# Strassen's scheme for the first product of three batches, in a float32 attention and ELU feed-forward kernel

## The chip, the cores and the metric

The kernel runs on one core of a Trainium2 chip. The metric is the device time of one execution in microseconds. Five engines work side by side, each through its own list of instructions: TensorE (PE in the profile, with the weight loads as PEld), VectorE (DVE), ScalarE (ACT), GpSimd (POOL) and SyncE (SP), which starts most transfers. They wait for each other through semaphores.

## The reference, cut to what matters

```python
B, N, C = (4, 6080, 256)                    # q, k, v: four batches
n_tokens, d_model, d_ff = (24320, 256, 2048)

def _attn_ref(q, k, v, tau):
    qn = q / (np.linalg.norm(q, axis=1, keepdims=True) + 1e-06)
    kn = k / (np.linalg.norm(k, axis=1, keepdims=True) + 1e-06)
    s = kn.transpose(0, 2, 1) @ qn / tau    # 256 x 256 per batch: attention over channels
    a = softmax(s)                          # by rows, with 1e-9 under the fraction
    return v @ a

x = _attn_ref(q, k, v, tau).reshape(24320, 256)
h = x @ w_in                                # 256 -> 2048
g = where(h > 0, h, exp(min(h, 0)) - 1)     # ELU
out = g @ w_out                             # 2048 -> 256
```

All of it is float32. w_in and w_out arrive as float64 and are converted on the chip.

## The kernel before

Each batch has its own 256 x 256 attention matrix. The kernel never forms v @ a: it multiplies the matrix into w_in (a tile `pw`, 256 x 2048 per batch, kept as `wp`) and then computes h = v @ wp. So the work per batch is a gram matrix k^T q with the column norms, a softmax, the product of a and w_in, and two large products.

For TensorE every float32 operand x is kept as two float32r tiles: hi, the cast of x, and lo = x - hi. One product is then three matmuls, hi hi, hi lo and lo hi (lines 423 to 425 and 461 to 465). The function `split` (lines 114 and 115) makes the two: a cast on ACT and a subtraction on DVE.

The 6080 tokens of a batch are cut into 12 chunks (8 of 512 and 4 of 496 columns), 48 in all. A chunk takes 16 steps, one for each 128 rows of the hidden layer. In a step `h_item` makes `ph` from `vt` (the chunk of v) and `wp` with 6 matmuls, `elu` makes `e` from it on ACT and DVE, `split_g` makes the pair `g`, and three steps later `out_item` adds g times w_out into the two banks `po` with 6 matmuls. ELU has two forms that alternate in most chunks: Relu(-h), Exp(-.), and a maximum (lines 434 to 436), or Exp, a clamp and a maximum (lines 438 to 440).

The first four chunks are interleaved while the weights are being converted. From then on chunk follows chunk. Side work is entered in a table of steps by hand: the groups of rows of the next batch's gram (load, square, add to `acc`, split, matmuls, which `fine` puts between the second product's matmuls), its softmax, its `pw`. Up to the first steps after the first four chunks, TensorE, DVE and ACT run in program order; after that a scheduler sets the order. The pool "w" has three PSUM banks, "gram" two and "o" three. GpSimd does almost nothing.

## Time and profile before

| What | Value |
|---|---|
| timed runs | 2165.70 and 2166.98 us, median 2166.34 |
| span of the profiled execution | 2163.4 us; the page gives no other time of it, the two timed runs are 2.3 and 3.6 us above it |
| busy share of the span | PE 100%, weight loads 88%, DVE 71%, ACT 68%, GpSimd 0% |
| granted TensorE clock | 1.00 in every stretch |

The rows that the prediction quotes are of five kinds. The page has the busy time of each engine and the chain of work that ended last, with its shares by engine. A row of stretches has a start and an end in us, its length, and for PE, PEld, DVE, ACT and POOL the busy time and the count of instructions, then the granted clock, the DMA share and GB/s. A row of the timeline has start, duration, engine, line, operation and tiles. A row of groups has line, engine, operation, tiles, shape and count, then busy time in us and mean duration in ns, and behind the second bar the idle time before them with what ended it. A row of DMA issues has the number of issues, the size of each and the us until it landed. L with a number is the line of the kernel. Batch 1's chunks begin near 593 us, batch 2's near 1128 and batch 3's near 1663.

### The profile page before, as it was taken

The numbers are of one execution on the slowest core, as the hardware profiler recorded it, in microseconds if no ns is written. First come the engines' busy times: TensorE is split into PE (matmuls) and PEld (weight loads), VectorE is DVE, ScalarE is ACT, GpSimd is POOL, SyncE is SP. The second block draws the span as 40 slices with busy tenths as digits, with TensorE's granted clock in tenths as the row PEclk, the third lists the DMA queues.
The fourth block names the chain that finished last, engine by engine and source line by source line (L and its number), as shares of the span: only waits on it lengthen the run. The fifth ranks groups of instructions, "written<-read, shape, count | busy, mean of one in ns | idle before, by whom it ended". The sixth has DMA issues, their size and how long they took to land.

```text
span 2163.4 us, 27196 instructions
## 1 busy us (share of the span) xinstructions
PE 2158.6 (100%) x10240; PEld 1911.9 (88%) x10240; DVE 1527.0 (71%) x2358; ACT 1469.1 (68%) x2422; POOL 3.3 (0%) x11
## 2 busy tenths in 40 slices
PE   9999999999999999999999999999999999999999
PEld 8888888899888888889988888888998888888998
DVE  7987777778766776776776677667776666666665
ACT  6877777667666666666766666666776666666665
POOL 0000000000000000000000000000000000000000
PEclk9999999999999999999999999999999999999999
DMA  9320222221111111111111112111112000000000
GB/s 357 107 78 30 78 69 68 68 65 49 59 38 50 49 59 49 59 58 46 39 59 39 49 50 68 49 58 49 56 31 67 20 30 27 23 20 11 20 10 20
DMA packets 62532, 120.77 MB, mean 56 GB/s; under 512 B 6208, under 2 KB 16064, under 8 KB 62400
## 3 DMA queue, kind: packets, MB, share of 16 engines
q1 hardware_dynamic: 62256, 118.91, 16.6%
q8 instruction: 80, 1.31, 0.2%
q14 instruction: 52, 0.43, 0.1%
q10 hardware_dynamic: 144, 0.13, 0.0%
HBM read 92.01 MB, written 27.00 MB: 55 GB/s over the span
## 4 chain that ended last, share of the span: by engine, by line
PE 100%; ACT 0%; DVE 0%; issue 0%
PE po L465 15%; PE po L463 15%; PE ph L423 15%; PE po L461 15%; PE ph L424 15%; PE ph L425 15%; PE gram L203 3%; PE gram L549 2%; PE gram L210 1%; PE pw L374 1%; PE pw L373 1%; PE pw L375 1%; PE pe L549 0%; PE pw L370 0%; PE pd L222 0%; PE pt L337 0%
## 5 line engine op out<-in xcount | busy, mean ns | idle before, releaser
L114 ACT CAST g<-e 128x512 fp32r<-128x512 f32 (+1 forms) x768 | 469.6, 611 | 483.5 <-DVE e L440 281.6
L115 DVE TENSOR_TENSOR g<-e,g 128x512 fp32r<-128x512 f32 (+1 forms) x768 | 525.6, 685 | 323.0 <-ACT g L114 295.6
L465 PE MATMUL po<-g,wo 128*128 128x512 f32 (+1 forms) x1536 | 579.3, 377 | 0.0
L463 PE MATMUL po<-g,wo 128*128 128x512 f32 (+1 forms) x1536 | 579.2, 377 | 0.0
L461 PE MATMUL po<-g,wo 128*128 128x512 f32 (+1 forms) x1536 | 578.9, 377 | 0.0
L423 PE MATMUL ph<-vt,wp 128*128 128x512 f32 (+1 forms) x1472 | 555.4, 377 | 0.0
L425 PE MATMUL ph<-vt,wp 128*128 128x512 f32 (+1 forms) x1472 | 554.5, 377 | 0.0
L424 PE MATMUL ph<-vt,wp 128*128 128x512 f32 (+1 forms) x1472 | 554.5, 377 | 0.0
L436 DVE SCALAR_TENSOR_TENSOR e<-e,ph 128x512 f32<-128x512 f32 (+1 forms) x416 | 283.2, 681 | 242.5 <-ACT e L435 241.9
L434 ACT ACTIVATE e<-ph 128x512 f32<-128x512 f32 (+1 forms) x416 | 246.6, 593 | 129.1 <-PE ph L425 114.4
L461 PEld LDWEIGHTS po<-g,wo 128*128 128x128 f32 x1536 | 290.3, 189 | 37.9 <-DVE scr L478 0.2
L463 PEld LDWEIGHTS po<-g,wo 128*128 128x128 f32 x1536 | 290.3, 189 | 37.8
L465 PEld LDWEIGHTS po<-g,wo 128*128 128x128 f32 x1536 | 290.7, 189 | 34.8 <-DVE g L115 0.3
L424 PEld LDWEIGHTS ph<-vt,wp 128*128 128x128 f32 x1472 | 278.2, 189 | 36.2
L425 PEld LDWEIGHTS ph<-vt,wp 128*128 128x128 f32 x1472 | 278.2, 189 | 36.1
L423 PEld LDWEIGHTS ph<-vt,wp 128*128 128x128 f32 x1472 | 278.2, 189 | 36.1
L435 ACT ACTIVATE e<-e 128x512 f32<-128x512 f32 (+1 forms) x416 | 261.3, 628 | 12.6
L440 DVE TENSOR_TENSOR e<-ph,e 128x512 f32<-128x512 f32 (+1 forms) x352 | 240.6, 684 | 10.4
L438 ACT ACTIVATE e<-ph 128x512 f32<-128x512 f32 (+1 forms) x352 | 207.9, 591 | 31.1 <-PE ph L425 29.2
L439 DVE TENSOR_SCALAR e<-e 128x512 f32<-128x512 f32 (+1 forms) x352 | 147.0, 418 | 20.7 <-ACT e L438 20.6
L182 DVE TENSOR_TENSOR acc<-acc,sq 128x1024 f32<-128x1024 f32 x84 | 102.6, 1221 | 12.2 <-ACT sq L181 11.1
L203 PE MATMUL gram<-qk 128*128 128x512 f32 x268 | 101.6, 379 | 0.0
(134 smaller groups left out, 1183.1 us busy)
## 6 DMA issues: line engine op xcount, KB each, us to landing
raw<-in_q_dram SPq DMA_DIRECT2D x76, 256.0 KB, 2.7
raw<-in_k_dram SPq DMA_DIRECT2D x76, 256.0 KB, 3.0
v<-in_v_dram SPq DMA_DIRECT2D x32, 512.0 KB, 3.6
out_dram<-o SPq DMA_DIRECT2D x56, 256.0 KB, 2.1
v<-in_v_dram SPq DMA_DIRECT2D x16, 496.0 KB, 3.5
out_dram<-o SPq DMA_DIRECT2D x31, 248.0 KB, 2.1
wraw<-w_scr SPq DMA_DIRECT2D x12, 512.0 KB, 3.2
room<-in_q_dram SPq DMA_DIRECT2D x16, 256.0 KB, 5.2
```

The lines of the kernel that those rows point to most:

```text
L114: nc.scalar.copy(hi, src)
L115: nc.vector.tensor_sub(lo, src, hi.bitcast(F32))
L423: nc.tensor.matmul(ph[:, 0:n], wp[kt][:, 0, fs], hi, start=(kt == 0), stop=False)
L424: nc.tensor.matmul(ph[:, 0:n], wp[kt][:, 0, fs], lo, start=False, stop=False)
L425: nc.tensor.matmul(ph[:, 0:n], wp[kt][:, 1, fs], hi, start=False, stop=(kt == KT - 1))
L434: nc.scalar.activation(ev, pv, AF.Relu, scale=-1.0)
L435: x = nc.scalar.activation(ev, ev, AF.Exp, scale=-1.0)
L436: y = nc.vector.scalar_tensor_tensor(ev, ev, -1.0, pv, op0=ALU.add, op1=ALU.max)
L440: y = nc.vector.tensor_tensor(ev, pv, ev, op=ALU.max)
L461: nc.tensor.matmul(o, wo[:, f, 0, ds], hi, start=first(c, f), stop=False)
L463: nc.tensor.matmul(o, wo[:, f, 1, ds], hi, start=False, stop=False)
L465: nc.tensor.matmul(o, wo[:, f, 0, ds], lo, start=False, stop=last(c, f))
```

## The change

For batches 1 to 3 the first product is no longer computed step by step. Four steps (512 rows of the hidden layer) are one unit, `fq`, and the unit's product is cut in 2 x 2 blocks: the product of weights and attention into A11, A12, A21, A22 (two halves of the 256 channels and two of the 512 rows) and the chunk of v into B11, B12, B21, B22 (two halves of the channels and two of the tokens). Strassen's scheme (in Winograd's form) then needs seven block products instead of eight: A11 B11, A12 B21, S3 T3, S2 T2, S1 T1, S4 B22 and A22 T4. The S are sums of A blocks and the T sums of B blocks. Each block product is 6 matmuls of 256 (or 248) columns.

- The sums S and T are made on GpSimd (`s_sum` once per unit of weights and batch, `t_sum` once per chunk), and split in hi and lo like everything else: T and the B blocks are cast on GpSimd, the S on GpSimd or ACT.
- The four results of a unit share partial sums. A11 B11 goes to `bank_a` and is copied on ACT into a second bank `bank_b` (one of two, `b_0` and `b_1`), in which S2 T2, S1 T1 and S4 B22 are accumulated one after the other; between them ACT copies the state of the bank to `u2` and `u4` in SBUF. S3 T3 and then A22 T4 go to `bank_e`, and DVE adds its two states to u4 and u2. So e11 comes from bank_a, e12 from bank_b, e21 from u2 and e22 from u4.
- All steps use the ELU form with Relu and Exp. The cast of g, which ACT did, is done by GpSimd.
- Between the products stand eight pieces of the second product (`multiply_out`), of the unit before. The second product itself has the same matmuls as before.
- All five engines run in program order in this part. Side work is a list of tasks with assumed costs, from which `spend` takes what fits a budget at given places in a unit; matmuls of the side work go between those of the second product (`beside`). The assumed costs are numbers of the code, not measurements shown here. Adding to `acc` and some casts may go to either of two engines.
- Some tiles change their buffers: `aT` shares that of `acc`, `cv` that of `sq`, g is made in pairs with three buffers for four.

Three places show how the instructions stand now. On PE, one step of a 512-column chunk of batch 3 before: `ph` is the first product, `po` the second.

```order
L423 MATMUL ph<-vt_15129,wp_0_13661 128x512
L424 MATMUL ph<-vt_15129,wp_0_13661 128x512
L425 MATMUL ph<-vt_15129,wp_0_13661 128x512
L423 MATMUL ph<-vt_15129,wp_1_13662 128x512
L424 MATMUL ph<-vt_15129,wp_1_13662 128x512
L425 MATMUL ph<-vt_15129,wp_1_13662 128x512
L461 MATMUL po_0_15001<-g,wo 128x512
L463 MATMUL po_0_15001<-g,wo 128x512
L465 MATMUL po_0_15001<-g,wo 128x512
L461 MATMUL po_1_15002<-g,wo 128x512
L463 MATMUL po_1_15002<-g,wo 128x512
L465 MATMUL po_1_15002<-g,wo 128x512
```

On PE after, the first part of a unit of batch 3: `bank_a`, `bank_e` and `b_` are block products, with `t_` and `s_` the tiles of T and of the weights (some B blocks lie in a free place of an `s_` tile).

```order
L1093 MATMUL bank_a<-s_5093,s_4870 128x256 x6
L1093 MATMUL bank_e<-t_5094,s_4870 128x256 x6
L1116 MATMUL po_0_16291<-g_16539,wo 128x512
L1117 MATMUL po_0_16291<-g_16539,wo 128x512
L1118 MATMUL po_0_16291<-g_16539,wo 128x512
L1116 MATMUL po_1_16307<-g_16539,wo 128x512
L1117 MATMUL po_1_16307<-g_16539,wo 128x512
L1118 MATMUL po_1_16307<-g_16539,wo 128x512
L1093 MATMUL b_5086<-t_5094,s_4870 128x256 x6
L1093 MATMUL bank_a<-s_4774,s_4870 128x256 x6
L1116 MATMUL po_0_16697<-g_16599,wo 128x512
L1117 MATMUL po_0_16697<-g_16599,wo 128x512
```

The first product now comes in groups of six narrow matmuls, and S2 T2 into `b_5086` has two block products and two outs ahead of it, during which ACT has to copy bank_a there.

On ACT, a piece of batch 3 before, with ELU's two forms (L434 and L435, L438) and the cast of g (L114).

```order
L114 CAST g<-e 128x512
L438 ACTIVATE e<-ph 128x512
L114 CAST g<-e 128x512
L434 ACTIVATE e<-ph 128x512
L435 ACTIVATE e<-e 128x512
L114 CAST g<-e 128x512
L438 ACTIVATE e<-ph 128x512
```

On ACT after, one unit of batch 3 and the first instruction of the next: `held` has the tiles of u2, e12 and e21, `e_e_5091` is e11, `e_e_5092` e22 and `e_u_5090` u4.

```order
L1455 COPY b_5086<-bank_a 128x512
L1468 COPY held<-b_5086 128x512
L1175 ACTIVATE e_e_5091<-bank_a 128x512
L1176 ACTIVATE e_e_5091<-e_e_5091 128x512
L1476 COPY e_u_5090<-b_5086 128x512
L1175 ACTIVATE e_e_5092<-e_u_5090 128x512
L1176 ACTIVATE e_e_5092<-e_e_5092 128x512
L1175 ACTIVATE held<-b_5086 128x512
L1176 ACTIVATE held<-held 128x512
L1175 ACTIVATE held<-held 128x512
L1176 ACTIVATE held<-held 128x512
L1455 COPY b_5085<-bank_a 128x512
```

The casts are gone, the copies L1455, L1468 and L1476 are new, and the copy for a unit stands behind the last Exp of the unit before.

On GpSimd before, its last instructions: a constant and one memset for each of three batches.

```order
masks.py:199 AFFINE_SELECT ident<-ident 128x128
L169 MEMSET raw_23_4109 128x2x256
L169 MEMSET raw_23_8546 128x2x256
L169 MEMSET raw_23_13108 128x2x256
L891 UNCONDITIONAL_BRANCH
```

On GpSimd after, the end of one unit of batch 3 (the last cast of g), the sums and casts of T for the next chunk, and the casts of g of the unit in which they stand.

```order
L1182 CAST g_18250<-held 128x2x256
L1018 TENSOR_TENSOR tt_18292<-v_18260 128x256
L1019 TENSOR_TENSOR tt_18292<-v_18260 128x256
L1026 CAST t_4714<-tt_18292 128x2x256
L1020 TENSOR_TENSOR tt_18292<-tt_18292,v_18260 128x256
L1021 TENSOR_TENSOR tt_18292<-v_18260,tt_18292 128x256
L1026 CAST t_4714<-tt_18292 128x2x256
L1182 CAST g_18327<-e_e_5091 128x2x256
L1182 CAST g_18363<-e_e_5092 128x2x256
L1182 CAST g_18327<-held 128x2x256
L1182 CAST g_18363<-held 128x2x256
```

Four sums and two casts for T (`tt_`, `t_`) now stand once per chunk ahead of the cast of e11.

The diff, cut to what the prediction speaks of:

```diff
-        aT = work.tile([P, 2, KT, C], F32R, tag="aT", bufs=1, name=f"aT_{b}")
+        aT = work.tile([P, 2, KT, C], F32R, tag="acc", bufs=1, name=f"aT_{b}")
...
-    for i in range(M * FT + LAG, len(steps) + LAG):
-        take(i)
...
+    MATRICES = ("A11", "A22", "A12", "S1", "S2", "S3", "S4")
...
+    def s_sum(b, fq, k):
+        a21, a11, a22, a12, s1, s2, s3, s4 = (x_of(b, fq, y, y + 1) for y in range(8))
+        add, sub = nc.gpsimd.tensor_add, nc.gpsimd.tensor_sub
+        (
+            lambda: add(s1, a21, a22),
+            lambda: sub(s2, s1, a11),
+            lambda: sub(s3, a11, a21),
+            lambda: sub(s4, a12, s2),
+        )[k]()
...
+    def spend(engine, budget, now):
+        order = [(engine, 0), (engine, 1), *((x, y) for x in SHARED.get(engine, ()) for y in range(2)), (engine, 2), (engine, 3)]
+        for key in order:
+            queue = queues[key]
+            while queue and queue[0].ready(now, 0):
+                t = queue[0]
+                cost = t.cost if key[0] == engine else t.cost[engine]
+                if cost > budget:
+                    break
+                queue.pop(0)
...
+    def t_sum(c, k):
...
+            lambda: sub(t1, b12, b11),
+            lambda: sub(t3, b22, b12),
+            lambda: add(t2, t3, b11),
+            lambda: sub(t4, b21, t2),
...
+    def t_hi(c, k):
+        hn = half_of(c)
+        nc.gpsimd.tensor_copy(t_groups[c % 2][:, k : k + 2, 0, 0:hn], state["tt", c][:, k : k + 2, 0:hn])
+
+    def t_lo(c, k):
+        hn = half_of(c)
+        t = t_groups[c % 2][:, k : k + 2]
...
+    def product(bank, c, fq, a, t, begin=False):
+        hn = half_of(c)
+        w, m = s_tiles[fq][:, MATRICES.index(a)], operands[c, t]
+        hi, lo = (in_turns(m[:, x, 0:hn]) for x in range(2))
+        for j in range(2):
+            js = slice(j * P, j * P + P)
+            for k, (x, y) in enumerate(((0, hi), (0, lo), (1, hi))):
+                nc.tensor.matmul(
+                    bank[:, j, 0:hn],
+                    w[:, x, js],
+                    y,
+                    start=(begin and j == 0 and k == 0),
+                    stop=(j == 1 and k == 2),
+                    skip_group_check=True,
+                )
...
+    def multiply_out(count, now):
+        for _ in range(count):
+            if not outs:
+                return
+            item = outs.pop(0)
+            if item is None:
+                continue
+            for _ in out_matmuls(*item):
+                beside(now)
...
+    outs += [None] * 4
...
+    def relu_exp(e, h):
+        nc.scalar.activation(e, h, AF.Relu, scale=-1.0)
+        nc.scalar.activation(e, e, AF.Exp, scale=-1.0)
+
+    def largest(e, h):
+        nc.vector.scalar_tensor_tensor(e, e, -1.0, h, op0=ALU.add, op1=ALU.max)
+
+    def hi_part(g, half, e, hn):
+        nc.gpsimd.tensor_copy(g[:, :, 0, half, 0:hn], e)
+
+    def lo_part(g, half, e, hn):
+        nc.vector.tensor_sub(g[:, :, 1, half, 0:hn], e, g[:, :, 0, half, 0:hn].bitcast(F32))
...
+        x = task(SP, 0, lambda: vraw.__setitem__(d, load_v(d)), when=t + PERIOD, level=0)
+        for k in range(4):
+            x = task(POOL, 0.65, lambda k=k: t_sum(d, k), [x], when=t + PERIOD, level=0)
+            if k % 2 == 1:
+                y = task(POOL, 0.65, lambda k=k: t_hi(d, k - 1), [x], when=t + PERIOD, level=0)
+                task(DVE, 0.685, lambda k=k: t_lo(d, k - 1), [y], when=t + PERIOD, level=0)
+        for k, when in enumerate((2 * PERIOD, 3 * PERIOD, 3 * PERIOD + 1)):
+            y = task(POOL, 0.35, lambda k=k: b_hi(d, k), [x], when=t + when, level=0)
+            task(DVE, 0.415, lambda k=k: b_lo(d, k), [y], level=0)
...
+    PACE = PERIOD * 23 / NG
...
+                    adds.append(task(ADD, {DVE: 0.685, POOL: 1.19}, add, [s], level=0))
...
+        x = task(ACT, 1.9, root, [pn], level=1)
...
+        e = {name: t[:, :, 0:hn] for name, t in e_tiles.items()}
+        bank_a = ps.tile([P, 2, HF], F32, tag="w", bufs=WB, name="bank_a")
+        product(bank_a, c, fq, "A11", "B11", True)
+        bank_b = banks_b[u % 2]
+        va, vb = bank_a[:, :, 0:hn], bank_b[:, :, 0:hn]
+        nc.scalar.copy(vb, va)
+        bank_e = ps.tile([P, 2, HF], F32, tag="w", bufs=WB, name="bank_e")
+        ve = bank_e[:, :, 0:hn]
+        product(bank_e, c, fq, "S3", "T3", True)
+        multiply_out(2, now)
+        if before is not None:
+            before()
+        spend(ACT, 1.9, now)
+        spend(POOL, 4.3, now)
+        spend(DVE, 2.5, now)
+        product(bank_b, c, fq, "S2", "T2")
+        product(bank_a, c, fq, "A12", "B21")
+        multiply_out(1, now)
+        nc.scalar.copy(e["u2"], vb)
+        product(bank_b, c, fq, "S1", "T1")
+        relu_exp(e["e11"], va)
+        largest(e["e11"], va)
+        g1 = work.tile([P, 2, 2, 2, HF], F32R, tag="g", bufs=3, name="g1")
+        hi_part(g1, 0, e["e11"], hn)
+        spend(POOL, 1.3, now + 2)
+        multiply_out(2, now)
+        nc.scalar.copy(e["u4"], vb)
+        nc.vector.tensor_add(e["u4"], ve, e["u4"])
+        product(bank_b, c, fq, "S4", "B22")
+        spend(ACT, 1.25, now + 2)
+        lo_part(g1, 0, e["e11"], hn)
+        spend(DVE, 1.0, now + 2)
+        multiply_out(1, now)
+        product(bank_e, c, fq, "A22", "T4")
+        relu_exp(e["e22"], e["u4"])
+        largest(e["e22"], e["u4"])
+        multiply_out(2, now)
+        g2 = work.tile([P, 2, 2, 2, HF], F32R, tag="g", bufs=3, name="g2")
+        hi_part(g2, 1, e["e22"], hn)
+        nc.vector.tensor_add(e["u2"], ve, e["u2"])
+        relu_exp(e["e12"], vb)
+        relu_exp(e["e21"], e["u2"])
+        lo_part(g2, 1, e["e22"], hn)
+        largest(e["e12"], vb)
+        hi_part(g1, 1, e["e12"], hn)
+
+        def before(e=e, g1=g1, g2=g2, hn=hn):
+            largest(e["e21"], e["u2"])
+            hi_part(g2, 0, e["e21"], hn)
+            lo_part(g1, 1, e["e12"], hn)
+            lo_part(g2, 0, e["e21"], hn)
+
+        for y, g in ((2, g1), (0, g2)):
+            for j in range(2):
+                for dt in range(DT):
+                    outs.append((c, 4 * fq + y + j, g[:, j], dt))
```

More of the change, by code (lines that the diff above doesn't have):

```diff
@@ L284, in norms @@
                 )
+    def norms(parts):
+        pn = ps.tile([P, 2, C], F32, tag="w", bufs=WB, name="pn")
+        for _ in norm_matmuls(parts, pn):
+            pass
         W = C + 2 * KT
@@ L862, in channel_attention_then_elu_ffn, with __init__, ready @@
     in_order.close()
-    for i in range(M * FT + LAG, len(steps) + LAG):
-        take(i)
+    ACT, DVE, POOL, PE, SP, CAST, ADD = "act", "dve", "pool", "pe", "sp", "cast", "add"
+    queues = {(e, level): [] for e in (ACT, DVE, POOL, PE, SP, CAST, ADD) for level in range(4)}
+    class Task:
+        def __init__(self, fn, deps, when):
+            self.fn, self.deps, self.when, self.done, self.cost = fn, deps, when, None, 0.0
+        def ready(self, now, gap):
+            return self.when <= now and all(d.done is not None and d.done + gap <= now for d in self.deps)
@@ new lines, in task @@
+    def task(engine, cost, fn, deps=(), when=0, level=1):
+        t = Task(fn, tuple(d for d in deps if d is not None), when)
+        t.cost = cost
+        queues[engine, level].append(t)
+        return t
+    SHARED = {ACT: (CAST,), DVE: (ADD,), POOL: (CAST, ADD)}
+    def spend(engine, budget, now):
[8 more added lines that the diff above has]
+                queue.pop(0)
+                budget -= cost
+                if key[0] == engine:
+                    t.fn()
+                else:
+                    t.fn({ACT: nc.scalar.copy, DVE: nc.vector, POOL: nc.gpsimd.tensor_copy if key[0] == CAST else nc.gpsimd}[engine])
+                t.done = now
@@ new lines, in channel_attention_then_elu_ffn, with beside @@
+    running = []
+    def beside(now):
+        while True:
+            if not running:
+                for level in range(3):
+                    queue = queues[PE, level]
+                    if queue and queue[0].ready(now, 2):
+                        running.append((queue[0], queue.pop(0).fn()))
+                        break
+                else:
+                    return
+            t, parts = running[0]
+            if next(parts, None) is not None:
+                return
+            t.done = now
+            running.clear()
@@ L868 @@
+    before()
+    now = PERIOD * len(units)
+    while outs:
+        multiply_out(1, now)
+        spend(ACT, 9, now)
+    for queue in queues.values():
+        assert not queue
+    in_order.close()
 _INS = ["q", "k", "v", "tau", "moe_w_in", "moe_w_out"]
```

442 lines of the change are left out of this document (403 added, 39 removed).

## The prediction

> **What bounds the kernel now.** I read the page from the top: the busy times, the 40 slices, the chain that ended last.
>
> ```profile
> span 2163.4 us, 27196 instructions
> ...
> PE 2158.6 (100%) x10240; PEld 1911.9 (88%) x10240; DVE 1527.0 (71%) x2358; ACT 1469.1 (68%) x2422; POOL 3.3 (0%) x11
> ...
> PEclk9999999999999999999999999999999999999999
> ...
> PE 100%; ACT 0%; DVE 0%; issue 0%
> ```
>
> The chain is TensorE from end to end, at full granted clock. A busy PE alone proves little, since its rows overlap; the chain and the pace of its starts do. So next the stretches of batches 1, 2 and 3 (one row each), and the starts of matmuls in the timeline: the first and the last of 58 in a row with 512 columns, of 30 with 496, then one with 256 and its successor.
>
> ```profile
> 593.00:1128.00 535.00, 535.00 (x2555) 474.45 (x2554) 378.53 (x583) 363.71 (x600) 0.73 (x1) 1.00 0.16 51
> 1128.00:1663.00 535.00, 535.00 (x2556) 474.42 (x2555) 378.47 (x583) 363.65 (x600) 0.73 (x1) 1.00 0.16 51
> 1663.00:2163.00 500.00, 496.63 (x2326) 439.15 (x2324) 309.60 (x504) 314.30 (x531) 0.00 (x0) 1.00 0.06 20
> ```
>
> ```profile
> 1699.68 0.38 PE L423 MATMUL ph<-vt,wp 128*128 128x512 f32 x1
> ...
> 1711.98 0.38 PE L461 MATMUL po<-g,wo 128*128 128x512 f32 x1
> ...
> 2153.19 0.37 PE L423 MATMUL ph<-vt,wp 128*128 128x496 f32 x1
> ...
> 2159.25 0.37 PE L465 MATMUL po<-g,wo 128*128 128x496 f32 x1
> ...
> 1004.52 0.27 PE L210 MATMUL gram<-qk 128*128 128x256 f32 x1
> 1004.63 0.38 PE L465 MATMUL po<-g,wo 128*128 128x496 f32 x1
> ```
>
> 12.30 us over 57 starts is 0.2158 us for 512 columns, 6.06 over 29 is 0.209 for 496, and a 256-column matmul holds its successor for 0.11. In the batch rows PE is busy throughout, DVE 71% and ACT 68%. Only less PE work shortens this kernel, as long as the others keep up.
>
> **The change, part by part.** *PE.* I call a quarter of a chunk's first product (4 of its 16 steps) a unit: 36 chunks x 4 = 144 units, of which 96 have 512 columns and 48 have 496. A unit issued 24 matmuls for the first product and 24 for the second. Now the first takes 7 products x 2 halves x 3 = 42 matmuls of 256 (or 248) columns. A long run of such narrow matmuls, each with weights of its own, is not in the trace. The nearest is in the norms: two of 256 columns, then four of 2 columns, whose weight loads stand in the second fence.
>
> ```profile
> 519.18 0.38 PE L274 MATMUL pn<-acc_split,ones_r 128*128 128x256 f32 x2
> ```
>
> ```profile
> 519.29 0.53 PEld L278 LDWEIGHTS pn<-ones_r,acc_split 128*128 128x128 f32 x4
> ...
> L278 PEld LDWEIGHTS pn<-ones_r,acc_split 128*128 128x128 f32 x12 | 1.6, 192 | 0.0
> ```
>
> Four loads of 0.192 in 0.53 us follow each other every (0.53 - 0.192)/3 = 0.113 us although their matmuls are nearly empty. So a narrow matmul costs 0.109 by L210's pace, or up to 0.113 if the loads set it; below that nothing speaks for 256, and for 248 in proportion 0.1056. I take 0.111 for both, because loads and matmuls come out nearly equal.
> 512: before 48 x 0.2158 = 10.36, after 24 x 0.2158 + 42 x 0.111 = 9.84, saved 0.52; x 96 = 50. 496: before 10.03, after 9.68, saved 0.35; x 48 = 17. Together 67 us, between 55 (all at 0.113) and 86 (0.109 and 0.1056). Gram, softmax and the product of weights and attention keep their matmuls.
>
> *The other engines.* Their prices:
>
> ```profile
> L434 ACT ACTIVATE e<-ph 128x512 f32<-128x512 f32 x288 | 171.8, 596 | 81.2 <-PE ph L425 71.3
> L435 ACT ACTIVATE e<-e 128x512 f32<-128x512 f32 x288 | 182.4, 633 | 9.0
> L114 ACT CAST g<-e 128x512 fp32r<-128x512 f32 x512 | 315.1, 616 | 328.2 <-DVE e L440 186.8 <-DVE e L436 141.2
> L487 ACT COPY o<-po 128x512 f32<-128x512 f32 x56 | 31.9, 588 | 4.2 <-PE po L465 3.1
> L440 DVE TENSOR_TENSOR e<-ph,e 128x512 f32<-128x512 f32 x224 | 154.7, 691 | 7.2
> L115 DVE TENSOR_TENSOR g<-e,g 128x512 fp32r<-128x512 f32 x512 | 353.2, 690 | 216.5 <-ACT g L114 210.7
> L182 DVE TENSOR_TENSOR acc<-acc,sq 128x1024 f32<-128x1024 f32 x84 | 102.6, 1221 | 12.2 <-ACT sq L181 11.1
> L324 DVE TENSOR_TENSOR a<-gram,a 128x256 f32<-128x256 f32 x6 | 2.2, 414 | 0.0
> L323 ACT COPY a<-gram 128x256 f32<-128x256 f32 x6 | 1.9, 378 | 0.0
> L169 POOL MEMSET raw<- 128x512 f32 x3 | 2.1, 715 | 1516.7 <-DVE qk L115 1516.7
> L226 ACT ACT_TABLE_LOAD x4 | 5.1, 1283 | 0.1
> ```
>
> Per unit ACT gets four Relu (0.596), four Exp (0.633) and three copies out of PSUM (0.588): 6.7 us. A copy that ends in PSUM has no row; 0.378 (the 256-wide L323, half as much) and 0.616 bound it, and I take L487. DVE gets ten operations of 0.69: 6.9 us. GpSimd gets the four casts of g. Its only row of that width is the memset, 0.715, which reads nothing. For a cast, a sum of 256 columns or a cast of 512 in the block below I take 0.715 too; the ends are 0.414 (DVE's 256-wide sum) and 1.43 (twice the memset, a read and a write one after the other). The Trainium skill, "GPSIMD Engine Reference", section "Performance versus the Vector engine", gives 4497 ns for a two-input sum of 2048 columns, an estimate of 0.56 us for 256; no run here shows it, and with it the block below would be shorter.
>
> Totals below 9.84 are not enough, since all queues now run in program order: a late result holds what stands behind it. So I lay one unit of 512 columns without side work along PE's starts. PE: A11 0, S3 0.67, two outs 1.33, S2 2.63, A12 3.29, one out 3.96, S1 4.61, two outs 5.27, S4 6.57, one out 7.24, A22 7.88, two outs 8.55, end 9.84. A reader starts 0.19 after a block (a matmul's 0.27 less its 0.11, and 0.03).
> ACT: copy of A11 1.0 to 1.6 (S2 needs it at 2.63); u2 3.48 to 4.07 (S1 at 4.61); Relu and Exp e11 to 5.38; u4 5.46 to 6.05 (S4 at 6.57); after DVE's largest e11 and sum u4 (6.79; A22 at 7.88) e22 to 8.05, e12 to 9.28; e21 waits for DVE's sum u2 (9.46, the next S3 at 10.51) and ends at 10.72, which is 0.88 of the next unit, and the loop closes. DVE's rest (largest e12 and e21, two low parts) ends at 3.28 of the next unit; the outs that need them begin at 3.96. The three places for g let the cast of e22 (8.80) start when PE has done the unit's fourth out (8.07). Every wait of PE is met with 0.5 us or more to spare, so I cost these waits at nothing; the cover is the outs between the products, and each 0.1 us lost per unit would be 14 us.
>
> Side work: in the first 23 units of batches 1 and 2 the planner puts about one group of the next gram in each unit. PE grows by 4 x 0.2158 + 4 x 0.109 = 1.30 to 11.1; ACT by four operations to 9.2, DVE by two and a quarter chunk's low parts ((2 x 0.69 + 3 x 0.414)/4 = 0.66) to 8.9. DVE has 2.1 us free before largest e11 and takes three operations there. It fits. SyncE too issues in program order now; the chunk of v that GpSimd's sums read lands in 3.6 us.
>
> ```profile
> v<-in_v_dram SPq DMA_DIRECT2D x32, 512.0 KB, 3.6
> ```
>
> Its load is issued as soon as a buffer of "raw" is free, which in a gram unit is near 8.7 of the unit before (after DVE's side step): it lands at 1.2, ahead of the sums at 2.6. I cost it at nothing; without that cover it would add its lateness to the block of the third rival.
>
> One-offs: four empty places in the list of outs leave the second unit's S2 without cover: the wait for sum, Relu, Exp and copy (0.69 + 0.60 + 0.63 + 0.59) less 1.3 of products is about 1.2 us. Two norms in batches 2 and 3 each put two table loads (2.57 us) into a gap of 1.9 on ACT: 0.7 each. Two starting matmuls: 0.4. I write 5 us for these and 4 for small waits.
>
> Sum, on the profiled execution: 2163.4 - 67 + 9 = 2105.4. The timed runs lie 2.3 and 3.6 above its span (start and end around it); 2.9 at their median of 2166.3 gives **2108 us**. Its own range is 2088 (86 saved, few waits) to 2123.
>
> **The rivals.** *GpSimd and DVE take turns.* DVE's four low parts and two of the four maxima (e22, e21) have both inputs in SBUF: 6 x 0.69 = 4.14 us, and with the chunk's low parts 4.8. GpSimd's work is 4 x 0.715 plus a quarter of (6 x 0.715 + 3 x 0.38) = 4.2. If they could not run at once, 9.0 of 9.84 would be taken in a plain unit, and in a gram unit 1.38 more on DVE and 1.5 sums of 512 columns on GpSimd (1.22 each, as DVE's for 1024): 12.2 of 11.1. That is 1.1 x 46 = 51 us, and with 0.3 for a collision in each other unit, 29: 2188; at half overlap about 2148. Against it: nothing in the trace, for GpSimd is idle there. The Trainium skill, "SBUF — State Buffer", section "Who interferes with whom", states just this: a Vector instruction with two SBUF inputs and a GpSimd instruction that reads SBUF block each other, whoever comes second waits. By that rule this rival is the forecast; no run here shows it. The unit's order leaves gaps that absorb part of it. Chance 0.25.
>
> *GpSimd's block of sums holds DVE (slower).* Once per chunk four sums and two casts stand on GpSimd ahead of the cast of e11. The block starts near 2.6; DVE's low part of e11 waits behind it, and largest e22, sum u2, e21 and the copy for the next S2 wait behind that. The cast of e11 would start at 6.1, so 3.6 us cost nothing; 0.5 are free before largest e22 and 1.0 at S2: it decides from 5.1 us on. At 0.715 an operation the block is 4.3. At 1.2 it is 7.2, and three casts before and after it are 0.5 later each: PE waits 3.6 us in each of 36 chunks, 128 us, about 2236, 3% slower; at 1.43 it would be 2310. For it: no GpSimd row reads anything. Against: 0.715 already includes a whole pass of 512 columns, and the sums have 256. Chance 0.15.
>
> *The narrow matmuls don't pay.* At 24 x 0.2158/42 = 0.123 us each the saving is gone and 2175 stands. L274's pair in 0.38 us and the loads at 0.113 speak against. Chance 0.05.
>
> **How the numbers follow.** The forecast has 0.55; two per cent, 43 us, is about what a measurement here can tell from no change. Faster by over 2% (below 2123): the forecast, 0.55. Within: the dear matmuls and the turn-taking, less 0.02 for its worst: 0.28. Slower (above 2209.7): the block and that worst, 0.17. The range runs from 2086, the short ends of the prices, to 2225, past full turn-taking, leaving out most of the dear block.
>
> **What would show it.** Right: starts of the 42 narrow matmuls every 0.109 to 0.113 us, PE at 98% or more of the span, the three stretches above at 513, 513 and 478 us, the chain still on PE. Turn-taking: L1182 on GpSimd or L1185 on DVE well above 0.715 and 0.69 while others of DVE (L1179 on a PSUM bank) stay. The block: PE idle once per chunk, released by the copy of L1455, behind L1018 to L1026. Wrong: narrow matmuls at 0.12 and more; PE waiting at S4 or S1 in every unit, which would mean that ACT's copies are dearer than 0.6.

## The result, and the profile after

The changed kernel takes **2264.16 us** (median of 2262.38 and 2265.94) against 2166.34: a ratio of 1.0453, 95% interval 1.0423 to 1.0483. It is slower by 98 us where 58 us of gain were forecast. The profiled execution took 2265.94 us, its span is 2264.1.

The page of the changed kernel, its busy times, its granted clock and its chain:

```profile
span 2264.1 us, 34396 instructions
...
PE 2156.0 (95%) x12834; PEld 1961.7 (87%) x12834; DVE 1785.3 (79%) x2514; ACT 1543.3 (68%) x2624; POOL 850.7 (38%) x1063
...
PEclk9999999999999999999999999999999999999999
...
PE 55%; DVE 17%; POOL 16%; issue 6%; ACT 5%; DMA 0%; POOLq 0%; ACTq 0%; DVEq 0%
```

TensorE is no longer the chain from end to end: it holds 55%, DVE and GpSimd 33%. The three stretches (batches 1, 2 and 3, cut where each begins in this kernel), with the busy time of PE, PEld, DVE, ACT and POOL and the granted clock:

```profile
593.00:1168.60 575.60, 534.19 (x3418) 489.92 (x3417) 470.41 (x640) 393.14 (x687) 298.84 (x360) 0.98 0.15 49
1168.60:1739.70 571.10, 536.28 (x3420) 491.59 (x3419) 472.28 (x638) 392.00 (x683) 310.14 (x370) 0.98 0.15 48
1739.70:2264.00 524.30, 493.98 (x3201) 457.42 (x3199) 380.47 (x549) 329.36 (x559) 221.82 (x302) 0.98 0.07 24
```

They are 576, 571 and 524 us where 513, 513 and 478 were forecast. PE idles in each, and the mean clock is 0.98, not 1.00. The three largest waits of PE, in us in total, times and the longest:

```profile
PE bank_e L1093 <- DVE e_u L1477: 91.7, 48, 3.6
PE bank_e L1093 <- DVE held L1489: 5.1, 6, 1.6
PE b L1093 <- ACT held L1468: 2.1, 3, 1.3
```

Nearly all of it is one wait: A22 times T4 accumulates onto the bank that sum u4 reads (L1477, DVE's addition of `bank_e` to u4), and DVE makes that sum late. The timeline shows one place of it, the second unit of a chunk in the last batch: first GpSimd, then DVE, then PE.

```profile
2013.84 1.60 POOL L1182 CAST g<-held 128x512 fp32r<-128x512 f32 x2 [1.39 <-DVE held L1179]
2015.41 1.17 POOL L1018 TENSOR_TENSOR tt<-v 128x256 f32<-128x256 f32 x1
2016.54 1.18 POOL L1019 TENSOR_TENSOR tt<-v 128x256 f32<-128x256 f32 x1
2017.78 0.61 POOL L1026 CAST t<-tt 128x512 fp32r<-128x512 f32 x1
2018.35 0.73 POOL L1020 TENSOR_TENSOR tt<-tt,v 128x256 f32<-128x256 f32 x1
2019.15 1.06 POOL L1021 TENSOR_TENSOR tt<-v,tt 128x256 f32<-128x256 f32 x1
2020.28 0.61 POOL L1026 CAST t<-tt 128x512 fp32r<-128x512 f32 x1
```

```profile
2014.91 2.21 DVE L1185 TENSOR_TENSOR g<-held,g 128x512 fp32r<-128x512 f32 x2 [0.51 <-POOL g L1182]
2018.42 1.21 DVE L1031 TENSOR_TENSOR t<-tt,t 128x512 fp32r<-128x512 f32 x1 [1.30 <-POOL t L1026]
2020.92 0.69 DVE L1031 TENSOR_TENSOR t<-tt,t 128x512 fp32r<-128x512 f32 x1 [1.29 <-POOL t L1026]
2021.53 0.68 DVE L1179 SCALAR_TENSOR_TENSOR e_e<-e_e,bank_a 128x512 f32<-128x512 f32 x1
2022.13 0.69 DVE L1477 TENSOR_TENSOR e_u<-bank_e,e_u 128x512 f32<-128x512 f32 x1
```

```profile
2012.63 0.83 PE L1093 MATMUL bank_a<-s,s 128*128 128x256 f32 x6
2013.29 0.83 PE L1093 MATMUL bank_e<-t,s 128*128 128x256 f32 x6
...
2022.87 0.94 PE L1093 MATMUL bank_e<-t,s 128*128 128x256 f32 x6 [2.18 <-DVE e_u L1477]
...
2024.77 0.63 PE L1117 MATMUL po<-g,wo 128*128 128x512 f32 x1
```

The unit starts at 2012.63. GpSimd's block of sums for the next chunk runs from 2015.41 to 2020.89. The second low part of T (L1031) stands in DVE's queue ahead of largest e11 (L1179, DVE's maximum for e11) and sum u4 and can only start when the block ends; the two follow, and PE starts A22 at 2022.87, 2.36 us later than the forecast's timetable (2012.63 + 7.88). Two things make PE late here: DVE waits for a block that it did not need yet, and the block lasts 5.5 us, since three of its sums take 1.06 to 1.18 us where a subtraction of DVE was already under way. The other sum takes 0.73: it began just ahead of DVE's first L1031, and there DVE's operation took longer, 1.21 us against 0.69 for the second.

The last row shows a third loss: 1.9 us after PE has resumed, a matmul of 512 columns takes 0.63 us in place of 0.38. The row of windows says why; the column behind the five busy times is the granted clock, 0.50:

```profile
2025.00:2026.00 1.00, 1.00 (x4) 0.82 (x4) 0.82 (x2) 0.73 (x2) 0.61 (x1) 0.50 0.00 0
```

The groups of instructions show the collisions over the whole run (mean ns of one behind the busy time):

```profile
L1185 DVE TENSOR_TENSOR g<-held,g 128x512 fp32r<-128x512 f32 x192 | 194.5, 1049 | 49.6 <-POOL g L1182 49.6
L1179 DVE SCALAR_TENSOR_TENSOR e_e<-e_e,bank_a 128x512 f32<-128x512 f32 x96 | 65.4, 681 | 38.0 <-ACT e_e L1176 36.1 <-PE b L1093 1.7
```

```profile
L1182 POOL CAST g<-held 128x512 fp32r<-128x512 f32 x192 | 153.4, 823 | 136.9 <-DVE held L1179 136.9
L1182 POOL CAST g<-e_e 128x512 fp32r<-128x512 f32 x192 | 117.7, 613 | 404.3 <-DVE e_e L1179 399.4 <-PE bank_a L1093 2.5 <-PE po L1118 2.4
```

This is the sign named for turn-taking: the low parts of e12 and e21 (two inputs in SBUF, beside GpSimd's casts) take 1.05 us in place of 0.69, the maximum on a PSUM bank stays at 0.68.

To put a number on each, I took the gaps between successive matmul starts from 593 us on and subtracted the usual pace (0.2158 us for 512 columns, 0.209 for 496, 0.111 for 256 and 248): what lies behind an ended matmul is idle time, the rest I call stretched starts. That gives 115.3 us idle and 47.7 us of stretched starts; without both, the span would be 2101.1. The forecast had 2096.4 (2163.4 - 67) and 9 us of waits. Of the 47.7 us, some 36 lie in the 20 stretches that the record shows at a granted clock of 0.50 (the mean clock of 0.983 over the span comes to 38); the other 12 are single gaps of mostly 0.1 us at a clock of 1.00, so not all of it is slow clock.

### The profile page after: what moved, and what is told of

Its sections match the earlier page's. It is cut to its first block, busy times and chain, and to the rows that moved or that the text cites. A ratio compares the mean times of both kernels' runs of the same rounds, so it can differ in the third digit from the quotient of the medians.

```text
span 2264.1 us, 34396 instructions
## 1 busy us (share of the span) xinstructions
PE 2156.0 (95%) x12834; PEld 1961.7 (87%) x12834; DVE 1785.3 (79%) x2514; ACT 1543.3 (68%) x2624; POOL 850.7 (38%) x1063
## 4 chain that ended last, share of the span: by engine, by line
PE 55%; DVE 17%; POOL 16%; issue 6%; ACT 5%; DMA 0%; POOLq 0%; ACTq 0%; DVEq 0%
POOL g L1182 7%; PE b L1093 5%; PE po L1116 5%; PE po L1118 5%; PE bank_e L1093 5%; PE po L1117 5%; DVE e_e L1179 4%; PE bank_a L1093 4%; PE ph L428 3%; PE ph L430 3%; PE ph L429 3%; DVE qk L1295 3%; PE po L472 3%; PE po L468 3%; PE po L470 3%
## 5 line engine op out<-in xcount | busy, mean ns | idle before, releaser
L1116 PE MATMUL po<-g,wo 128*128 128x512 f32 (+1 forms) x1158 | 447.6, 387 | 0.8 <-POOL g L1182 0.8
L1118 PE MATMUL po<-g,wo 128*128 128x512 f32 (+1 forms) x1158 | 445.2, 384 | 0.4 <-DVE g L1185 0.4
L1117 PE MATMUL po<-g,wo 128*128 128x512 f32 (+1 forms) x1158 | 445.3, 385 | 0.0
L1093 PE MATMUL bank_e<-t,s 128*128 128x256 f32 (+1 forms) x1728 | 258.4, 287 | 98.7 <-DVE e_u L1477 91.7
L1093 PEld LDWEIGHTS bank_e<-t,s 128*128 128x128 f32 x1728 | 229.9, 198 | 129.2 <-DVE e_u L1477 116.4
L1185 DVE TENSOR_TENSOR g<-held,g 128x512 fp32r<-128x512 f32 (+1 forms) x288 | 283.7, 1021 | 73.3 <-POOL g L1182 73.3
L1182 POOL CAST g<-held 128x512 fp32r<-128x512 f32 (+1 forms) x288 | 228.4, 817 | 202.8 <-DVE held L1179 202.8
L1118 PEld LDWEIGHTS po<-g,wo 128*128 128x128 f32 x1158 | 223.7, 193 | 31.6 <-DVE g L1185 1.0
L1185 DVE TENSOR_TENSOR g<-e_e,g 128x512 fp32r<-128x512 f32 (+1 forms) x288 | 207.3, 720 | 52.7 <-POOL g L1182 42.7
L1093 PEld LDWEIGHTS b<-t,s 128*128 128x128 f32 x1728 | 233.4, 191 | 15.7 <-ACT held L1468 3.2
L1093 PE MATMUL b<-t,s 128*128 128x256 f32 (+1 forms) x1728 | 239.7, 275 | 3.0 <-ACT held L1468 2.1
L1175 ACT ACTIVATE e_e<-e_u 128x512 f32<-128x512 f32 (+1 forms) x144 | 90.3, 627 | 222.0 <-POOL g L1182 163.1
L1117 PEld LDWEIGHTS po<-g,wo 128*128 128x128 f32 x1158 | 225.2, 194 | 15.1
L1116 PEld LDWEIGHTS po<-g,wo 128*128 128x128 f32 x1158 | 224.9, 194 | 13.0 <-POOL g L1182 1.2
L1468 ACT COPY held<-b 128x512 f32<-128x512 f32 (+1 forms) x144 | 83.9, 583 | 169.0 <-PE b L1093 115.8
L1176 ACT ACTIVATE held<-held 128x512 f32<-128x512 f32 (+1 forms) x288 | 180.5, 627 | 9.1
L1176 ACT ACTIVATE e_e<-e_e 128x512 f32<-128x512 f32 (+1 forms) x288 | 180.5, 627 | 9.2
L115 DVE TENSOR_TENSOR g<-e,g 128x512 fp32r<-128x512 f32 (+1 forms) x192 | 132.2, 688 | 48.9 <-ACT g L114 47.6
```

Of the source, the lines that this page charges most:

```text
L115: nc.vector.tensor_sub(lo, src, hi.bitcast(F32))
L1093: nc.tensor.matmul(bank[:, j, 0:hn], w[:, x, js], y, start=(begin and j == 0 and k == 0), stop=(j == 1 and k == 2), skip_group_check=True,)
L1116: yield nc.tensor.matmul(o, wo[:, f, 0, ds], hi, start=begin, stop=False)
L1117: yield nc.tensor.matmul(o, wo[:, f, 1, ds], hi, start=False, stop=False)
L1118: yield nc.tensor.matmul(o, wo[:, f, 0, ds], lo, start=False, stop=end)
L1175: nc.scalar.activation(e, h, AF.Relu, scale=-1.0)
```

## The experiments

Each time below is compared with the kernel before, at 2165.6 to 2165.7 us, run on the same chip. A unit of 512 columns without side work was forecast at 9.84 us.

**1. The low parts of T later.**

```
- task(DVE, 0.685, lambda k=k: t_lo(d, k - 1), [y], ...)
+ task(DVE, 0.685, lambda k=k: late.append(lambda: t_lo(d, k - 1)), [y], ...)
...
+ while late: late.pop(0)()      # in the next unit, behind before()
```

> The whole of the change, but the two low parts of T that DVE makes once per chunk (L1031) stand one unit later in its queue, behind the four operations that close a unit, not ahead of largest e11 and sum u4 of the unit in which GpSimd makes the sums. Theory of the order (DVE waits there for the end of GpSimd's block, and with it sum u4 and PE): the long units (13.25 us against 9.87 in the last batch) go, PE's idle time falls from 115 us to 30 to 50, the time to 2150-2190. Theory of turn-taking (operations of DVE and GpSimd stretch each other and eat the unit's margin): the block is as long as before, the cast of e11 still stands behind it, and the time stays within 20 us of 2264.

Measured: 2194.72 us, 1.0131 (1.0114 to 1.0148): 69 us less than the change, 5 us above the range expected by the theory of the order. In the last batch a chunk of 512 columns takes 39.6 us (read, as all lengths of units and chunks here, from one largest e11 to the next); in the change it was 42.0 or 43.6, and four units of the forecast are 39.4. So the wait of DVE for the block was the order's doing. Idle time is 76 us, more than expected, and most of it lies in the units with gram work, where DVE now meets another GpSimd operation. The timeline of one such place:

```profile
1320.15 3.40 POOL L1278 TENSOR_TENSOR acc<-acc,sq 128x512 f32<-128x512 f32 x2
1320.65 3.45 DVE L1031 TENSOR_TENSOR t<-tt,t 128x512 fp32r<-128x512 f32 x2
1324.02 0.41 DVE L1051 TENSOR_TENSOR s<-v,s 128x256 fp32r<-128x256 f32 x1
1324.36 1.28 DVE L1295 TENSOR_TENSOR qk<-raw,qk 128x512 fp32r<-128x512 f32 x2
```

Two subtractions of 512 columns take 3.45 us while GpSimd makes two sums of squares; right after, two others of the same size take 1.28.

**2. The wait filled with matmuls.**

```
+ if fq == 1 and c + 1 < NCH:
+     for _ in range(11):
+         nc.tensor.matmul(banks_b[(u + 1) % 2], ones_r, wo[:, 0], start=False, stop=False, ...)
  product(bank_e, c, fq, "A22", "T4")
```

> The whole of the change, and in the second unit of each chunk PE issues 11 matmuls of 512 columns (2.4 us) into a bank that is free then, ahead of A22, where it stood idle for 2.2 us. If the granted clock of 0.50 that follows such a wait comes from PE's idle time, it goes: the wait is no shorter, the 48 us of slow matmuls shrink to about 10, and the time falls by 25 to 40 us, to 2224-2239. If the clock falls for another reason, the time stays at 2264 or rises by the 0.2 us per chunk that the fill is too long (7 us).

Measured: 2250.36 us, 1.039 (1.0375 to 1.0406); a fall of 14 us, not 25 to 40. The mechanism is there: the stretched starts fall from 47.7 to 14.3 us, of which under 2 us are left at a clock of 0.50, and the mean clock rises from 0.983 to 0.999. The fill cost more than I reckoned: the added matmuls take 89 us of pace and replace only 72 us of idle time. 17.8 - 33.4 = -15.6, which is the difference of the two spans (2248.6 and 2264.1).

**3. No block of T sums** (the block's tasks dropped, the T of the first Strassen chunk used for all).

> Leaves out part of the computation: the T sums, their casts and low parts are made for the first Strassen chunk alone and used for all others, so GpSimd's block and DVE's wait for it are gone; all casts of g, the B parts and the gram's work on GpSimd stay. Theory of the order: the 82 us of idle time in the second units and most of the 48 us at a low clock go, 2264 - 82 - 37 = about 2145 (2130-2160). Theory of turn-taking: the four casts of a unit still collide with DVE's low parts, and more than half of the loss stays, 2190 or more.

Measured: 2141.53 us, 0.9887 (0.9872 to 0.9902), as the theory of the order had it. This does not clear turn-taking, though: with the block, the collisions that lengthen it are gone too, and so is the work of the block itself.

**4. GpSimd beside DVE in the kernel before.** A cast, a difference or a sum on GpSimd, twice per step, on the tile that ScalarE and DVE split.

```
+ nc.gpsimd.tensor_copy(to[:, x, 0 : CH - 16].bitcast(F32R), e[:, 0 : CH - 16])    # chunks 36 to 39
+ nc.gpsimd.tensor_sub(to[:, x, 0 : CH // 2 - 8], hi, lo)                          # chunks 40 to 43
+ nc.gpsimd.tensor_add(to[:, x, 0 : CH // 2 - 8], hi, lo)                          # chunks 44 to 47
```

> The kernel before, with two extra operations on GpSimd per step of the last batch that nobody reads, on the tile e that ScalarE and DVE split at that time: casts of 496 columns in chunks 36 to 39, differences of 248 columns in 40 to 43, sums of 248 in 44 to 47. If DVE with two inputs in SBUF and GpSimd take turns: the subtraction L115 rises from 0.69 to 0.8-1.1 us on the mean in the last batch, while L440 with one input in PSUM stays at 0.67-0.69, and GpSimd's own operations take 0.6 us free and 1 us or more where they meet L115. If not: all of DVE's rows stay. The time stays near 2166 in both cases (PE has the work, DVE is at 61% there).

The groups of DVE in the last batch, first of the kernel before, then of this run:

```profile
L115 DVE TENSOR_TENSOR g<-e,g 128x512 fp32r<-128x512 f32 x128 | 88.7, 693 | 78.0 <-ACT g L114 76.6
L440 DVE TENSOR_TENSOR e<-ph,e 128x512 f32<-128x512 f32 x64 | 44.3, 692 | 2.2
L439 DVE TENSOR_SCALAR e<-e 128x512 f32<-128x512 f32 x64 | 26.9, 420 | 0.0
```

```profile
L115 DVE TENSOR_TENSOR g<-e,g 128x512 fp32r<-128x512 f32 x128 | 116.0, 906 | 78.1 <-ACT g L114 76.7
L440 DVE TENSOR_TENSOR e<-ph,e 128x512 f32<-128x512 f32 x64 | 44.3, 692 | 2.2
L439 DVE TENSOR_SCALAR e<-e 128x512 f32<-128x512 f32 x64 | 44.3, 692 | 0.0
```

The subtraction with both inputs in SBUF goes from 0.693 to 0.906 us on the mean, the operation with one input in PSUM stays at 0.692. Turn-taking is real, and it depends on where the inputs lie. L439, which reads one SBUF tile and writes SBUF, is held as well: its single durations are 0.41 to 0.42 or 0.81 to 0.94 us. The time was 2201.64 us in one run, 36 above the kernel before: I had expected none, since DVE was at 61% there. PE's largest wait in this run is for ScalarE's copies of the output:

```profile
PE po L461 <- ACT o L487: 18.9, 10, 2.0
```

That these copies are late because ScalarE's casts ahead of them wait for DVE is likely, but no run shows it.

**5. Low parts that read PSUM.** The order is untouched and the collisions of the low parts are gone. The bank holds other values, so the result is not the reference's. The low parts of T read that bank too.

```
- nc.vector.tensor_sub(g[:, :, 1, half, 0:hn], e, g[:, :, 0, half, 0:hn].bitcast(F32))
+ other = banks_b[state["other"]][:, :, 0:hn]
+ nc.vector.tensor_sub(g[:, :, 1, half, 0:hn], other, g[:, :, 0, half, 0:hn].bitcast(F32))
```

> The whole of the change in its order and with all its waits, but every low part of the Strassen chunks (the four of g per unit and the two of T per chunk) subtracts from a PSUM bank in place of the tile in SBUF, so that DVE has one input in SBUF there; the values are wrong, sizes and waits are the same. If turn-taking lengthens the block: GpSimd's sums of 256 columns fall from 1.06-1.17 to 0.73 us, the block from 5.4 to 4.2 us, PE's wait in the second units from 2.2 to about 1.0 us, and with 35 x 1.2 = 42 us of idle time and some of the slow clock the time falls to 2185-2225. What is left of the wait (1 us) is the order's. If the order alone made the loss, the sums stay above 1 us and the time within 15 us of 2264.

Measured: 2168.97 us, 1.0016 (1.0006 to 1.0026); 95 us less, more than the 40 to 80 expected. The second unit of a chunk in the last batch:

```profile
1927.84 0.74 POOL L1018 TENSOR_TENSOR tt<-v 128x256 f32<-128x256 f32 x1
1928.54 0.73 POOL L1019 TENSOR_TENSOR tt<-v 128x256 f32<-128x256 f32 x1
1929.33 0.61 POOL L1026 CAST t<-tt 128x512 fp32r<-128x512 f32 x1
1929.90 0.73 POOL L1020 TENSOR_TENSOR tt<-tt,v 128x256 f32<-128x256 f32 x1
1930.71 0.73 POOL L1021 TENSOR_TENSOR tt<-v,tt 128x256 f32<-128x256 f32 x1
1931.51 0.61 POOL L1026 CAST t<-tt 128x512 fp32r<-128x512 f32 x1
...
1934.09 0.94 PE L1094 MATMUL bank_e<-t,s 128*128 128x256 f32 x6 [0.96 <-DVE e_u L1480]
```

All sums take 0.73, the block 4.28 us in place of 5.48, and PE waits 0.96 in place of 2.18. Both fit one sum: from the block's end DVE needs 1.98 us to A22 (2022.87 - 2020.89), so a block that starts 2.78 into the unit costs nothing up to 7.88 - 1.98 - 2.78 = 3.1 us, and then its whole excess: 1.2 and 2.4 us for the two blocks (the waits in the rows are 0.2 shorter, as they count from the modelled end of the matmul before). The rest of the 95 us came from the units with gram work (mostly 10.6 to 11.2 us here, 11.5 to 12.1 in the change) and from the clock: with waits of 1 us the stretched starts fell from 47.7 to 14.1 us, those at a clock of 0.50 from 36 to 5.

**6. The block cut in two** (T1 and T3 in the second unit, T2 and T4 in the third, low parts behind that of e11).

> The whole of the change, correct in full, with the block of sums cut in two: T1 and T3 with their cast in the second unit of a chunk, T2 and T4 with theirs in the third, and each low part of T on DVE behind the low part of e11 in the same unit, where sum u4 no longer waits for it. By the order and the prices measured (1.17 + 1.17 + 0.61 = 2.95 us a half), the half block ends before DVE comes to it, no unit is held by it, and the time is near that without the block, 2141: 2130-2165. If the sums hurt by their collisions with DVE wherever they stand, or if DVE is full in the units with gram work, 2175-2200 as with the late low parts.

Measured: 2205.66 us, 1.0185 (1.017 to 1.02): the second case, 6 us above its range. The last batch runs at 39.6 us per chunk, but the third unit takes 14.4 us in the gram half.

**7. Neither the block nor the collisions** (3 and 5 together).

> Both causes taken out at once: no T block (as in e3, part of the computation left out) and the four low parts of g read a PSUM bank (as in e5, values wrong). If the two together are the whole loss, what is left is the forecast: PE's zero-wait time of 2101 us plus few waits, 2105-2120 with the clock above 0.995. If a third cause lies in the units with gram work (DVE's or ScalarE's queue full by itself), PE still waits there and the time stays above 2125.

Measured: 2123.59 us, 0.9804 (0.9789 to 0.9819), between the two marks. Its stretches:

```profile
593.00:1115.80 522.80, 516.25 (x3420) 481.85 (x3418) 404.16 (x612) 392.49 (x689) 224.49 (x297) 1.00 0.17 54
1115.80:1637.10 521.30, 517.06 (x3419) 483.10 (x3418) 403.74 (x608) 388.47 (x682) 230.47 (x305) 1.00 0.16 53
1637.10:2121.70 484.60, 478.76 (x3200) 448.25 (x3198) 326.20 (x523) 326.99 (x556) 151.71 (x235) 1.00 0.08 26
```

Units take 9.87 us alone and 11.18 with a group of the gram (forecast 9.84 and 11.1); 15.5 us idle and 4.9 of stretched starts are left, the largest part around the softmax. So these two causes are nearly the whole loss, and they multiply. From 2123.6, the block alone costs 45 us (2169.0), the collisions of the low parts alone 18 (2141.5), both 141 (2264.2): of the 141, 77 us appear only when both are there. What collides is then the block that DVE waits for (35 blocks, each 1.2 us longer, make 42 us), and with waits of 2 us the clock is at 0.50 more often (36 us in place of 5).

**8, 9 and 10. The sums of squares on DVE.** Three kernels, all with the low parts of T one each in the third and fourth unit. Run 8:

```
- SHARED = {ACT: (CAST,), DVE: (ADD,), POOL: (CAST, ADD)}
+ SHARED = {ACT: (CAST,), DVE: (ADD,), POOL: (CAST,)}
...
- task(DVE, 0.685, lambda k=k: t_lo(d, k - 1), [y], when=t + PERIOD, level=0)
+ task(DVE, 0.685, lambda k=k: t_lo(d, k - 1), [y], when=t + (k + 3) // 2 * PERIOD, level=0)
...
- spend(DVE, 2.5, now)
+ spend(DVE, 3.2, now)
```

> Correct in full. The sums of squares of the gram (L1278), 1.6 us each on GpSimd where they hold DVE's operations with two SBUF inputs, go to DVE alone (0.69 each, DVE's share of a unit's first slot 3.2 us in place of 2.5), and the two low parts of T stand one each in the third and the fourth unit of a chunk. If what held DVE in the gram units was GpSimd's sums, DVE gains more than the 0.69 it takes on: 2120-2150, faster than before. If DVE was simply full there, it gets worse than with the late low parts: 2195 or more.

> As the run with all sums of squares on DVE, but with shares of 2.5 us in the first slot of a unit (ahead of largest e11) and 1.4 us in the second (ahead of largest e22). If sum u4 is what PE waits for, less work ahead of it is better: 2115-2145, below the other. If sum u2 and the copy for the next S2 are as late, it is the same or worse by up to 20 us.

> Correct in full. As the run with the sums of squares on DVE (low parts of T one each in the third and fourth unit, DVE's share 3.2 us), but GpSimd keeps its part of those sums (71 of 92 in the change). It tells what their place alone is worth: if GpSimd's sums hold DVE in the gram units, the gram units stay at 11.5 to 15 us and the time is 2185-2205, 25 to 45 us above 2160; if the spreading of the low parts made the gain, it is within 10 us of 2160.

Measured: 2159.85 us for the first, 0.9976 (0.9966 to 0.9986); 2177.53 for the other shares, 1.0054 (1.0039 to 1.0069); 2185.98 with GpSimd's part kept, 1.0091 (1.0074 to 1.0108). The first is 26 us below the last, so work given to the busier engine made the kernel faster: each sum takes 0.76 us on DVE (92 sums) but 1.62 on GpSimd, and DVE's subtractions beside it are held (3.45 us for 1.28 in the place of run 1). Still, 2159.85 is 10 us above the range expected for it. (In the last of the three, GpSimd made 47 of the 92, not the 71 of the expectation, as DVE's larger share took more.) The middle one is the second case of its expectation, and its largest wait is the one named there, for sum u2 (L1489):

```profile
PE bank_e L1093 <- DVE held L1489: 26.0, 28, 3.1
```

**11 and 12. The shared casts on ScalarE, and then the block cut in two.** `POOL: ()` in the line above and `spend(ACT, 2.5, now)` in place of 1.9; then also the cut.

> Correct in full. As the run with the sums of squares on DVE, and GpSimd also makes none of the casts that it shared with ScalarE (19 of S and of the input weights, around the softmax); ScalarE's share of a unit's first slot grows from 1.9 to 2.5 us. If these casts hold DVE in the units around the softmax (the low parts L837 took 0.9 to 1.1 us there against 0.69), some 5 to 10 us go: 2148-2157. If ScalarE becomes late for the copies that S1 and S4 wait for, 2165-2185.

> Correct in full. As the fastest so far (sums of squares on DVE, shared casts on ScalarE alone), and GpSimd's block of T sums is cut in two, T1 and T3 in the second unit and T2 and T4 in the third, their low parts one unit later each. In the fastest so far the cast of e11 still stood behind the whole block; where that held PE (the units of 12 to 13 us around the softmax) 5 to 15 us go: 2136-2147. If the waits there come from the softmax's own chain, the time stays at 2148-2155.

Measured: **2151.45 us** for the first, 0.9934 (0.9919 to 0.9948), the fastest of those that do the whole work, 0.7% ahead of the kernel before and less than the 2% that the prediction counts as a change. The second missed both of its ranges: 2169.72, 1.0019 (1.0009 to 1.0028). In the gram halves its third unit waits for sum u4 in every chunk, 0.8 to 2.0 us and mostly 1.1. The likely reason, which no run shows alone, is that the half blocks meet DVE's fullest stretch (its queue ahead of largest e11) in two units of a chunk, where the whole block met it in one.

## Why the prediction was wrong

- *The narrow matmuls* were right. Six of 256 columns take 2013.29 - 2012.63 = 0.66 us, 0.11 each. A unit without waits takes 9.87 (9.84 forecast), and PE's saving without waits is 62 us of the 67. The rival that they don't pay fell.
- *The timetable of a unit* was right where nothing else is in it: with the block away, the units of the last batch run at 9.87 and every wait is met. ScalarE's prices (L1175, L1176, L1455, L1468, L1476) are within 0.04 us of those taken.
- *The step that failed* is the block's place: "DVE's low part of e11 waits behind it", and "it decides from 5.1 us on". The first wait is another: DVE's own low parts of T, which the sum has only as work (2 x 0.69 us in the 0.66 us per unit of a chunk's low parts), stand ahead of largest e11 and sum u4 and wait for the block's end. The block decides from 3.1 us. At the forecast's own 4.3 us it costs 1.2 us per chunk, where the forecast put it at nothing, and run 5 has just that block and that cost. I counted their 0.69 us each and not what they wait for. The rival of the block was right that the block makes it slower, and had a chance of only 0.15 for want of this wait. That its 2236 is near the result is luck: it came from a block of 7.2 us that holds the cast of e11, where the block lasts 5.5, holds the low parts of T, and the clock adds its part.
- *GpSimd's price* was right for an operation alone: 0.715 taken, 0.73 (sum of 256) and 0.61 (cast of 512) measured. Beside DVE's subtractions it is 1.06 to 1.18. So the rival of turn-taking is true as well, and I weighed the two as if only one could hold. The rule of the Trainium skill, "SBUF — State Buffer", section "Who interferes with whom", that two SBUF inputs on Vector and a GpSimd read exclude each other, agrees with run 4: L115 rose by 0.21, L440 by nothing. It agrees with run 5 too, where all sums of the block take 0.73.
- *The gram units* were forecast at 11.1 and are 11.18 without collisions, 11.5 to 12.1 with them: GpSimd's sums of squares were taken at 1.22 us and took 1.62 on the mean, and in the place of run 1 they held two subtractions of DVE by 2.2 us.
- *The clock* was not in the forecast at all: some 36 us at 0.50, nearly a quarter of the miss. "Each 0.1 us lost per unit would be 14 us" is too low for waits of 2 us.
- *One-offs* of 5 us: run 7 keeps 20 us of idle time and stretched starts, the largest part around the softmax; the forecast had 9.

Together: 4.7 (pace) + 106.3 (idle beyond 9) + 47.7 (stretched starts, the clock among them) = 158.7 = 2264.1 - 2105.4.

## What to carry to other kernels

When queues run in program order, list for each moved instruction what it waits for, not only how long it takes: an operation with slack of its own holds everything behind it. Prefer to give GpSimd work where DVE reads PSUM or rests, and price it with the DVE time that it blocks; sums moved from the idler engine to the busier one were a gain here. Before PE is left to wait, ask whether the wait nears 2 us: in the last batch a wait of 2.2 us cost another 1.6 us where the half clock followed (chunks of 43.6 us against 42.0).

## What the hardware did that I had not expected

- *Short waits slow the clock.* The Trainium skill, "TensorE: Matmul & The Clock Gate", section "Part 1: The HAM clock gate (the "warmup" mystery)", has the clock at half after an idle window of about 3.4 us; here the trace shows it after less, 1.95 us idle. In the changed kernel all stretches at 0.50 begin on one grid of 3.41 us (1979.86 and 2024.23 are 13 steps apart) and last one step, two of them two. Each of these 20 (a last one lies at the kernel's very end) follows a step in which PE had no matmul under way for 1.95 us or more; behind a step with 1.83 us or less none begins. So equal waits differ: of ten waits of 1.9 to 2.2 us in the last batch from 1800 us on, five lie whole or nearly so in one step and are followed by the half clock, five are split by the grid and are not. The rows of windows show one of each, cut at the grid: PE is idle for 2.06 us in the first step, for 0.92 and 1.12 in the third and fourth.

```profile
2020.81:2024.23 3.42, 1.36 (x9) 1.31 (x10) 2.59 (x4) 1.29 (x3) 0.69 (x2) 1.00 0.09 31
2024.23:2027.64 3.41, 3.41 (x15) 3.06 (x14) 3.23 (x5) 2.84 (x5) 1.19 (x2) 0.50 0.00 0
2061.77:2065.19 3.42, 2.50 (x15) 1.93 (x13) 1.98 (x3) 0.51 (x1) 2.44 (x4) 1.00 0.40 134
2065.19:2068.60 3.41, 2.29 (x14) 2.13 (x15) 2.68 (x5) 2.19 (x4) 0.71 (x2) 1.00 0.00 0
2068.60:2072.02 3.42, 3.42 (x27) 3.25 (x26) 2.73 (x5) 1.95 (x5) 2.03 (x3) 1.00 0.00 0
```

  From 593 us on, over the changed kernel and the twelve runs together, 49 of 50 steps with 1.84 us or more idle were followed by the half clock. That fewer and filled waits remove it is shown by runs 2 and 5; no run moved a wait on the grid on purpose.
- *A one-input operation is held too.* L439, SBUF to SBUF with constants, rose from 0.420 to 0.692 us on the mean beside GpSimd's work, more in proportion than the two-input L115. The Trainium skill, "SBUF — State Buffer", section "Who interferes with whom", lists tensor_scalar among the operations that can take both ports; I had read it for two-input operations only.
- *Both sides pay.* A subtraction of 256 columns on GpSimd took 1.17 for 0.73 us, and the two low parts of DVE beside it 2.21 for 1.29: the work of the two engines added up nearly as if on one (two sums of 0.73 and the 1.29 make 2.75 us; the rows from 2014.91 to 2017.72 make 2.81).
- *248 columns are no faster than 256.* Narrow matmuls of both widths started every 0.111 us on the mean, where 0.1056 had been the prediction's low end for 248.
